# Windowed attention and a gated MLP on one core: when w_out's rows are requested, and the order of units 4 to 7 on TensorE

## The chip, the cores and the metric

The kernel runs on one core of a Trainium2 chip. The metric is device time in microseconds of one execution; lower is better. A core has five engines that run side by side, each through its own list of instructions in order: TensorE (PE in the profile; PEld is its weight load), VectorE (DVE), ScalarE (ACT), GpSimd (POOL) and SyncE (SP). They wait for one another through semaphores. DMA transfers are requested by an engine's list and carried out by 16 DMA engines that all queues share. SyncE's requests go through the profile's queue q1, GpSimd's through q0. Matmuls read SBUF and write PSUM, which has eight banks of 128 x 512 float32; VectorE and ScalarE bring results back to SBUF.

## The reference, cut to what matters

```python
# q, k, v: 4 batches x 8 heads x 768 positions x 64, float32
scores = q @ k.T / 8                       # per head
keep = (key < 4) | ((0 <= row - key) & (row - key < 128))   # 4 sinks, a window of 128
a = softmax(where(keep, scores, -1e9))
x = (a @ v), heads side by side            # 3072 tokens x 512
h = x @ w_in                               # 512 x 2048
g = h * sigmoid(beta * h)                  # beta per column
out = g @ w_out                            # 2048 x 512, float32
```

Only blocks on the band of 128 and the sinks' columns of the score matrix have to be computed.

## The kernel before, in words

**Tiles and units.** The 3072 tokens are cut into 8 tiles of 384, two per batch. The attention of a tile is done in four *units*, each one pair of heads: unit n belongs to tile n // 4. Odd tiles are the second half of a batch; their units also attend to the four sinks, for which `k_sink` and `v_sink` are kept apart. A unit needs q and k of its rows (`load_qk`, two transfers of 192 KB), cast to bf16 (`cast`), transposed on TensorE (`transpose_in`, or `transpose_first` for units 0 to 3) and copied back as `qkT`; then scores, one or two exponentials on ScalarE, a mask on VectorE (L733, L771), the product with v (`attend`, L789 and L800), division by the row sums (`normalise`, L809 and L811), and a transpose into `xT` (`transpose_out`). Units 8 and up have their results transposed by DMA, units 12 and up their inputs too (`land_qk`, `turn`).

**The MLP.** For each tile, 16 hidden blocks of 128 columns (`hidden`, L844: four matmuls of 384 columns each), a tanh on ScalarE (L852) and a product on VectorE (`gate`, L865) give g; then 3 x 16 products with w_out (`project`, L879) make the tile's 384 output rows: for each of three row groups t, sixteen blocks m are summed in one bank. The three groups use the banks acc0 and acc1 in turn. Hidden blocks need w_in, which comes in four quarters of four blocks (`load_w_in`), and products need w_out, which comes in eight transfers of two blocks (`load_w_out`). Both are cast from float32 to bf16 on the way, which is why GpSimd requests them. All of it is loaded once, during tiles 0 and 1.

**What sets the order.** The program is recorded as nodes with costs by `op`, each for one engine, and `Prog.order` plans them: for every engine it takes, of the nodes whose inputs are ready, the one that can start first, in five rounds between which the landings of DMA transfers are worked out anew (`landings`) from sizes, rates, weights and the numbers in `QUEUE`, `TAIL` and `late`. The plan only fixes the order on each engine; on the chip semaphores decide the time. Where the planner sees TensorE idle ahead of the first products, it puts in *fillers*, matmuls of ones into a bank that is free (L871). An argument `after` of a node makes it wait for the writers of the tiles named: `load_w_out(0, 2, [("w_in", 0, 12)])` waits until the last quarter of w_in has landed. `seq` keeps the loads on one queue in program order.

**The part in question** is tile 0's MLP and tile 1's attention, 17 to 50 us. SyncE requests q and k of units 4 to 7 and the float32 v of tile 1 (`load_v32`) when w_in's second quarter has landed. GpSimd casts them, casts v (`cast_v`), and between these requests w_out; it also requests the sinks' keys (`load_sink_keys`, two transfers of 8 KB into `k_rows`), which TensorE transposes (L632) into `k_sink`. Units 8 to 11 are loaded by SyncE into the stage buffers of units 0 to 3, each after one of w_out's transfers: unit n after the transfer that brings block 2n - 12. `Q_COPY` says which engine copies the transposed q of units 0 to 3 out of PSUM.

Of the kernel before, what the change touches and what calls it, by code (L numbers as in the profile page):

```python
# [9 lines left out]
B, H, S, D = 4, 8, 768, 64  # L10
NSINK, WINDOW = 4, 128
DM, DF, NOUT = 512, 2048, 512
# [6 lines left out]
TT = 384  # L19
NT = NTOK // TT  # L20
NU = 4 * NT
NM = DF // 128
# [23 lines left out]
NEG = -1.0e6  # L46
PE_MASK = 4

Q_COPY = ("act", "act", "dve", "dve")

# [319 lines left out]
def bass_streamingllm_window__then__act_swish_beta_kernel(  # L370
# [29 lines left out]
    xT = sb("xT", (128, 4, NTOK), BF16)  # L400
# [6 lines left out]
    ident = sb("ident", (128, 128), BF16)  # L407
# [6 lines left out]
    v_stage = sb("v_stage", (128, 3, H, D), F32)  # L414
# [5 lines left out]
    k_rows = sb("k_rows", (NPAIR, NSINK, 2, D), BF16)  # L420
# [19 lines left out]
    def pe(n):  # L440
        return {"busy": 2.5 + n / 2.4, "lag": 260.0}
# [7 lines left out]
    def transfer(size, rate, busy=470.0, weight=1.0):  # L449
        return {"busy": busy, "lag": size / rate, "weight": weight}  # L450
# [69 lines left out]
    def place(n):  # L520

        return n // 8, n % 4, n // 4 % 2, n % 4
# [7 lines left out]
    def load_qk(n, x, after=(), queue="sp"):  # L530
        _, _, half, pb = place(n)
        name = "qk"[x]
        s = rows_of((q, k)[x], n, 1, half, 3)
        d = stage[name][pb][:, :, 3 * half:3 * half + 3, :].rearrange("p h c d -> p h (c d)")
        op(queue, lambda e: e.dma_start(d, s), w=[(name + "_stage", pb, half)], after=after,  # L535
           dma=f"{name}{pb}_{half}", seq="loads " + queue, **transfer(2 * TT * D * 4, 330 if n < 4 else 290, 520.0))

    def load_v32(T, x, c, after=()):

        eng = "sp"  # L540
        kb = 3 * T + c
        src = v[0, 4 * x:4 * x + 4, kb * 128:kb * 128 + 128, :].rearrange("h p d -> p h d")
        op(eng, lambda e: e.dma_start(v_stage[:, c, 4 * x:4 * x + 4, :], src), w=[("v_stage", x, c)], after=after,
           dma=f"v{x}{c}", seq="loads " + eng, **transfer(4 * 128 * D * 4, 230, 520.0))

    def cast_v(n, eng="gp", after=()):
        z, T = n % 4, n // 4
        op(eng, lambda e: e.tensor_copy(v_aug[:, z, :, 3 * T:3 * T + 3, 0:D].rearrange("p h c d -> p c h d"),
                                        v_stage[:, :, 2 * z:2 * z + 2, :]),
           r=[("v_stage", z // 2, c) for c in range(3)], after=after,  # L550
           w=[("v", z, 3 * T + c, hh) for c in range(3) for hh in range(2)],
           **({"busy": 460.0, "lag": 100.0} if eng == "gp" else dve(450.0)))
# [46 lines left out]
    def load_w_out(m, ms, after=()):  # L599
        op("gp", lambda e: e.dma_start(w_out16[:, m:m + ms, :], w_out_src[:, m:m + ms, :]), after=after,  # L600
           w=[("w_out", mm) for mm in range(m, m + ms)],
           dma=f"wo{m}", **transfer(ms * 128 * NOUT * 4, 416, 740.0, 3.0))

    def load_sink_keys(after=()):
        for hh in range(2):
            src = k[:, :, 0:NSINK, :].rearrange("b (g h) s d -> h (b g) s d", h=2)[hh]
            op("gp", lambda e, hh=hh, src=src: e.dma_start(k_rows[:, :, hh, :], src),
               w=[("k_rows", hh)], after=after, dma=f"sk{hh}", busy=650.0, lag=300.0, weight=0.4)
# [18 lines left out]
    def sink_keys():  # L627

        bank16 = tr_ps[:, :].bitcast(BF16)
        with P.together("pe"):  # L630
            for s in range(NSINK):
                op("pe", lambda e, s=s: nc.tensor.transpose(  # L632
                    bank16[:, s * NPAIR:(s + 1) * NPAIR],
                    k_rows[:, s, :, :].rearrange("n h d -> n (h d)"), ident[0:NPAIR, 0:NPAIR]),
                   r=[("k_rows", 0), ("k_rows", 1), "ident"], w=["tr"], **pe(60))
        src = bank16[:, 0:NSINK * NPAIR].rearrange("x (s n) -> x n s", s=NSINK)
        for hh in range(2):
            rows = slice(64 * hh, 64 * hh + 64)
# [238 lines left out]
    def project(T, t, m, bank, name, eng="act", cols=slice(0, NOUT), queue="sp"):  # L877
# [25 lines left out]
       w=["beta_stage"], dma="beta", busy=500.0, lag=100.0)  # L903
# [6 lines left out]
    for c in range(3):  # L910
        load_v32(0, 1, c)
    op("act", lambda e: e.activation(scratch[:, :], ones32[:, 0:1], AF.Exp, bias=0.0, scale=1.0),
       r=["ones32"], w=["scratch"], busy=1500.0)
# [24 lines left out]
    cast(3)  # L938
    load_w_in(4, 4, [("k16", 0)])
    cast_v(2)  # L940
    cast_v(3)
    load_w_in(8, 4, [("v", 3, 0, 0)])
    load_w_in(12, 4, [("v", 3, 0, 0)])
    for n in range(4):
        if n < 2:
            transpose_first(n + 2)
        if n < 3:
            first_scores(n + 1)
        if n == 2:
            for y in range(4, 8):  # L950
                for x in range(2):
                    load_qk(y, x, [("w_in", 0, 4)])
                if y % 2 == 1:
                    for c in range(3):
                        load_v32(1, y // 6, c)
            masks(0, range(6), [("v", 3, 0, 0)])
            load_sink_keys([("v", 3, 0, 0)])
            load_w_out(0, 2, [("w_in", 0, 12)])
        bank = (acc[1], "acc1") if n < 3 else (h_ps[:, 0, :], "h0")
        attend(n, *bank)  # L960
        normalise(n, *bank)
# [19 lines left out]
    for s in range(-2, S_END + NM):  # L981
        i = block_of(s) if 0 <= s < S_END else None
        if i is not None:
            hidden(i, 3 if i < 2 else 0)
        if i == 2:
            P.fillers.append((filler(0), [ones_made], P.nodes[-2]))
        later = []
        for n, step in AGENDA.get(s, ()):
            if step == "in" and n < XBAR:
                transpose_in(n, eng="act" if n in (5, 7) else "dve")  # L990
            if step == "b" and n // 4 != 2:
                scores_at_once(n, 0 if n < 8 else 2)
# [12 lines left out]
        if s in casts:  # L1005
            cast(casts[s])
        if s == 3:
            for n in range(4, 8):
                cast_v(n, "gp")
        if s == 0:  # L1010
            for m in range(2, 8, 2):
                load_w_out(m, 2, [("k_stage", 1, 1)])
        if s == 2:
            for m in range(8, NM, 2):
                load_w_out(m, 2, [("k_stage", 1, 1)])
            for n in range(8, 12):
# [73 lines left out]
```

## Time and profile before

| | us |
|---|---|
| median of 3 runs | 229.56 |
| the three runs | 228.48, 229.56, 229.59 |
| the profiled execution | 228.67 |
| its span, first to last instruction | 226.7 |
| TensorE busy in the span | 215.9 |

The granted TensorE clock of the span reads 1.00. The profile gives the span alone; the profiled execution's own time is some 2 us longer, which lies around the span. In a timeline a row is a run of like instructions on one engine: start, length, engine, line, what it writes and reads, and in brackets how long the engine had been idle and what ended that. The line of GpSimd's or SyncE's request tells when a transfer was asked for, not when it landed; the time to landing is given apart. Transfers that matter here, requested and landed: w_in at 8.90, 11.68, 13.74, 14.47, landed 6.3, 6.2, 7.0 and 9.4 us later; unit 4's q at 17.85 (6.2) and k at 18.26 (6.5); the sinks' keys at 16.65 and 17.16 (7.6 and 7.3).

### The profile page before, as it was taken

What the parts mean: (1) busy time and instruction counts of PE and PEld (TensorE: products, weight loads), DVE (VectorE), ACT (ScalarE), POOL (GpSimd) and SP (SyncE); (2) the same over time, 40 slices, a digit from 0 to 9 for tenths busy, and PEclk for the clock granted to TensorE, in tenths of its full rate; (3) what the DMA queues carried; (4) which work ended last, traced back from release to release, by engine and by line L of the source; (5) the groups of instructions that cost most, each with busy time, mean ns of one, the idle gap of its engine ahead of it and who ended that gap; (6) DMA issues with size and microseconds to landing.
All of it is one profiled execution on the core that took longest, in us unless ns stands there. A gap on an engine that the chain in (4) does not pass through costs nothing.

```text
span 226.7 us, 4386 instructions
## 1 busy us (share of the span) xinstructions
PE 215.9 (95%) x1716; PEld 121.4 (54%) x1743; DVE 132.4 (58%) x261; ACT 140.4 (62%) x204; POOL 125.1 (55%) x193
## 2 busy tenths in 40 slices
PE   7899948999999999999999999999999999999995
PEld 4466625464555555555555555455555555555454
DVE  4776735558996566777766655555566563443200
ACT  3678855527776768666767676666656765555310
POOL 6681793589997697998979497877300000000000
DMA  5999999999999998999999999999901102110122
GB/s 158 262 196 200 263 247 201 239 261 158 107 117 112 166 118 116 124 130 146 172 115 154 102 138 137 123 155 136 141 20 58 53 21 64 46 49 0 61 78 93
DMA packets 98388, 29.68 MB, mean 131 GB/s; under 512 B 84912, under 2 KB 95424, under 8 KB 98368
## 3 DMA queue, kind: packets, MB, share of 16 engines
q0 software_dynamic: 55888, 10.52, 61.0%
q1 hardware_dynamic: 42304, 18.75, 37.2%
q8 instruction: 13, 0.21, 0.4%
q10 hardware_dynamic: 176, 0.14, 0.2%
q14 instruction: 7, 0.06, 0.1%
HBM read 27.32 MB, written 6.29 MB: 148 GB/s over the span
## 4 chain that ended last, share of the span: by engine, by line
PE 78%; DMA 13%; POOL 3%; SPq 2%; issue 2%; ACT 0%; ACTq 0%; POOLq 0%
PE hs_ps L844 33%; PE acc L879 32%; DMA w_out<-in_moe_w_out_dram 6%; PE hs_ps L800 4%; PE hs_ps L753 4%; DMA q_stage<-in_q_dram 3%; DMA w_in<-in_moe_w_in_dram 3%; SPq L535 2%; DMA k_stage<-in_k_dram 2%; POOL w_out L600 2%; PE hs_ps L879 2%; PE hs_ps L789 1%; PE hs_ps L719 1%; POOL qk L649 1%; PE hs_ps L742 1%
## 5 line engine op out<-in xcount | busy, mean ns | idle before, releaser
L852 ACT ACTIVATE th<-hs_ps,beta_half 128x384 f32<-128x384 f32 x120 | 68.7, 581 | 50.8 <-PE hs_ps L844 49.5
L879 PE MATMUL acc<-w_out,g 128*128 128x512 bf16 x341 | 93.1, 380 | 4.9 <-DMA w_out<-in_moe_w_out_dram 3.2
L844 PE MATMUL hs_ps<-xT,w_in 128*128 128x384 bf16 x480 | 94.4, 326 | 0.4 <-DVE g L865 0.2
L865 DVE SCALAR_TENSOR_TENSOR g<-th,hs_ps 128x384 bf16<-128x384 f32 x120 | 65.2, 551 | 35.6 <-ACT th L852 33.8
L844 PEld LDWEIGHTS hs_ps<-xT,w_in 128*128 128x128 bf16 x480 | 45.4, 98 | 35.8 <-DVE g L865 1.2
L879 PEld LDWEIGHTS acc<-w_out,g 128*128 128x128 bf16 x368 | 33.4, 98 | 34.9 <-DMA w_out<-in_moe_w_out_dram 4.4
L765 ACT ACTIVATE E<-hs_ps 128x1920 bf16<-128x1920 f32 (+1 forms) x24 | 39.9, 1661 | 4.8 <-PE hs_ps L753 4.6
L569 POOL DMA_DIRECT2D land<-in_q_dram x40 | 30.5, 766 | 15.2 <-DVE rden L809 15.2
L771 DVE TENSOR_TENSOR E<-E,mask 128x1536 bf16<-128x1536 bf16 x24 | 23.2, 967 | 26.3 <-ACT E L765 26.3
L569 POOL DMA_DIRECT2D land<-in_k_dram x40 | 30.5, 765 | 0.0
L578 POOL DMA_DIRECT2D v_aug<-in_v_dram x40 | 30.5, 764 | 0.0
L887 ACT ACTIVATE out_sb<-acc 128x512 f32<-128x512 f32 x23 | 13.6, 595 | 13.2 <-PE acc L879 13.1
L800 PE MATMUL hs_ps<-v_aug,E 128*128 128x65 bf16 x348 | 17.4, 193 | 0.1
L800 PEld LDWEIGHTS hs_ps<-v_aug,E 128*128 128x128 bf16 x348 | 15.7, 97 | 2.9 <-issue 1.6
L811 DVE TENSOR_TENSOR o_norm<-hs_ps,rden 128x384 bf16<-128x384 f32 x29 | 16.1, 557 | 1.1
L726 ACT ACTIVATE E<-hs_ps 128x768 bf16<-128x768 f32 x16 | 12.5, 807 | 2.4 <-PE hs_ps L719 2.4
L753 PE MATMUL hs_ps<-qkT 64*128 64x128 bf16 (+2 forms) x176 | 12.1, 253 | 0.0
L789 PE MATMUL hs_ps<-v_sink,E 128*128 128x130 bf16 x48 | 9.3, 219 | 0.0
L753 PEld LDWEIGHTS hs_ps<-qkT 64*128 64x128 bf16 x176 | 6.0, 94 | 5.8 <-issue 5.1
L809 DVE RECIPROCAL rden<-hs_ps 128x6 f32<-128x6 f32 x29 | 5.6, 192 | 4.7 <-PE hs_ps L800 4.7
L649 POOL CAST qk<-k_stage 128x384 bf16<-128x384 f32 x12 | 6.2, 515 | 3.0 <-DMA k_stage<-in_k_dram 2.9
L649 POOL CAST qk<-q_stage 128x384 bf16<-128x384 f32 x8 | 4.1, 517 | 6.4 <-DMA q_stage<-in_q_dram 6.4
(67 smaller groups left out, 135.5 us busy)
## 6 DMA issues: line engine op xcount, KB each, us to landing
out_dram<-out_sb SPq DMA_DIRECT2D x23, 256.0 KB, 2.6
q_stage<-in_q_dram SPq DMA_DIRECT2D x12, 192.0 KB, 5.8
k_stage<-in_k_dram SPq DMA_DIRECT2D x12, 192.0 KB, 6.0
w_in<-in_moe_w_in_dram POOLq DMA_DIRECT2D x4, 512.0 KB, 6.6
w_out<-in_moe_w_out_dram POOLq DMA_DIRECT2D x8, 256.0 KB, 9.7
land<-in_q_dram POOLq DMA_DIRECT2D x40, 48.0 KB, 3.4
land<-in_k_dram POOLq DMA_DIRECT2D x40, 48.0 KB, 3.8
v_aug<-in_v_dram POOLq DMA_DIRECT2D x40, 48.0 KB, 3.3
```

The source lines that it names most:

```text
L569: op("gp", lambda e, d=d, s=s: e.dma_start(d, s), w=[("land", pb, half, x, hh)], after=after, dma=f"l{pb}{half}{x}{hh}", **transfer(TT * D ...
L578: op("gp", lambda e, d=d, s=s: e.dma_start(d, s), w=[("v", pb, 3 * half + c, hh) for c in range(3)], after=after, dma=f"lv{pb}{half}{hh}", ...
L753: op("pe", lambda e, at=at, w=w, kb=kb, qb=qb, nq=nq, hh=hh, rows=rows, bank=bank: e.matmul(hs_ps[:, of + 2 * hh + bank, at:at + w], keys_ ...
L765: op("act", lambda e: e.activation(dst, src, AF.Exp, bias=0.0, scale=SCALE), x=list(names), w=[("E", z, 0), ("E", z, 1)], **act(1920 if ha ...
L771: op("dve", lambda e: e.tensor_tensor(E[z][:, :, 0:768], E[z][:, :, 0:768], m.unsqueeze(1).to_broadcast([128, 2, 768]), ALU.mult), r=[("E" ...
L800: last=(x == len(kbs) - 1): e.matmul(av_ps[:, at + hh * D1:at + hh * D1 + D1], E[z][:, hh, col:col + 128], v_aug[:, pb, hh, kb, 0:D1], sta ...
L811: op("dve", lambda e: e.tensor_tensor(o_norm[o][:, :, :, :].rearrange("p m h d -> p (m h) d"), src[:, :, 0:D], rden[z][:, :].unsqueeze(2). ...
L844: op("pe", lambda e: e.matmul(bank, w_in16[:, c, m * 128:(m + 1) * 128], xT[:, c, T * TT:(T + 1) * TT], start=(c == 0), stop=(c == 3)), r= ...
L852: op("act", lambda e: e.activation(th[i % 3][:, :], bank, AF.Tanh, bias=0.0, scale=beta_half[:, m:m + 1]), x=[name], r=["beta"], w=[("th", ...
L865: op("dve", lambda e: e.scalar_tensor_tensor(g[T % 2][:, m, :], th[i % 3][:, :], 1.0, bank, ALU.add, ALU.mult), r=[("th", i % 3)], x=[name ...
L879: op("pe", lambda e: e.matmul(bank[:, 0:width], g[T % 2][:, m, t * 128:(t + 1) * 128], w_out16[:, m, cols], start=(m == 0), stop=(m == NM ...
L887: op("act", lambda e: e.activation(out_sb[z][:, 0:width], bank[:, 0:width], AF.Copy, bias=0.0, scale=0.5), x=[name], w=[("out_sb", z)], ** ...
```

## The change

1. `Q_COPY`: the q of units 2 and 3 is copied by ScalarE instead of VectorE.
2. w_out's first two blocks are requested when w_in's second quarter has landed, not its last.
3. w_out's other blocks: 2 to 7 are recorded with the casts of unit 7 and may go once k of unit 6 (blocks 2 to 5) or k of unit 7 (6 and 7) has landed; 8 to 15 once the last v of tile 1 has landed. Before, all of them could go once k of unit 5 had landed.
4. The sinks' keys are requested between casts of v, ahead of w_in's last two quarters, and their transposes wait for `xT` of unit 3.
5. The loads of units 4 to 7 keep their order (written out), and those of v wait for w_in's second quarter by name. The loads of units 8 to 11 are recorded two blocks later (s == 4 instead of 2) with the same `after`.
6. The planner's numbers for these transfers change: rates, weights, and a delay of 3300 for the q of unit 4. They act through the order alone.

The order that comes out differs on every engine. On TensorE the transposes of `k_rows` go before hidden block 3, unit 4's q transposes after block 11 and its k after block 13; no filler stands after the hidden layer; 4 products with w_out precede unit 6's transposes, and 24 (instead of 48) precede the first hidden matmul of tile 1. The transposes of unit 8, which preceded it, follow it. On GpSimd: request of blocks 0 and 1, casts of units 4 and 5, casts of v, casts of unit 6, request of blocks 2 and 3, casts of unit 7, requests of 4 to 7, casts of v, requests of 8 to 15.

```diff
-Q_COPY = ("act", "act", "dve", "dve")
+Q_COPY = ("act", "act", "act", "act")
...
            dma=f"{name}{pb}_{half}", seq="loads " + queue,
-           **transfer(2 * TT * D * 4, 330 if n < 4 else 290, 520.0))
+           late=3300.0 if (n, x) == (4, 0) else 0.0,
+           **transfer(2 * TT * D * 4, 290 if n > 3 else 180 if n == 1 else 330, 520.0, 5.0 if 4 <= n < 8 else 1.0))
...
-           dma=f"v{x}{c}", seq="loads " + eng, **transfer(4 * 128 * D * 4, 230, 520.0))
+           dma=f"v{x}{c}", seq="loads " + eng, **transfer(4 * 128 * D * 4, 230, 520.0, 0.55))
...
-           dma=f"wo{m}", **transfer(ms * 128 * NOUT * 4, 416, 740.0, 3.0))
+           dma=f"wo{m}", **transfer(ms * 128 * NOUT * 4, 350, 740.0, 3.0))
...
                    k_rows[:, s, :, :].rearrange("n h d -> n (h d)"), ident[0:NPAIR, 0:NPAIR]),
-                   r=[("k_rows", 0), ("k_rows", 1), "ident"], w=["tr"], **pe(60))
+                   r=[("k_rows", 0), ("k_rows", 1), "ident"], w=["tr"], after=[("xT", 0, 3)], **pe(60))
...
     cast_v(2)
+    load_sink_keys([("k16", 0)])
     cast_v(3)
...
         if n == 2:
-            for y in range(4, 8):
-                for x in range(2):
-                    load_qk(y, x, [("w_in", 0, 4)])
-                if y % 2 == 1:
-                    for c in range(3):
-                        load_v32(1, y // 6, c)
+            load_qk(4, 0, [("w_in", 0, 4)])
...
+            load_v32(1, 1, 2, [("w_in", 0, 4)])
             masks(0, range(6), [("v", 3, 0, 0)])
-            load_sink_keys([("v", 3, 0, 0)])
-            load_w_out(0, 2, [("w_in", 0, 12)])
+            load_w_out(0, 2, [("w_in", 0, 4)])
...
+        if s == 2:
+            load_w_out(2, 2, [("k_stage", 2, 1)])
+            load_w_out(4, 2, [("k_stage", 2, 1)])
+            load_w_out(6, 2, [("k_stage", 3, 1)])
         if s == 3:
             for n in range(4, 8):
                 cast_v(n, "gp")
-        if s == 0:
-            for m in range(2, 8, 2):
-                load_w_out(m, 2, [("k_stage", 1, 1)])
-        if s == 2:
-            for m in range(8, NM, 2):
-                load_w_out(m, 2, [("k_stage", 1, 1)])
+            load_w_out(8, 2, [("v_stage", 1, 2)])
+            load_w_out(10, 2, [("v_stage", 1, 2)])
+            load_w_out(12, 2, [("v_stage", 1, 2)])
+            load_w_out(14, 2, [("v_stage", 1, 2)])
+        if s == 4:
             for n in range(8, 12):
                 for x in range(2):
                     load_qk(n, x, [("w_out", 2 * n - 12)])
```

More of the change, by code (lines that the diff above doesn't have):

```diff
@@ L535, in load_qk @@
         op(queue, lambda e: e.dma_start(d, s), w=[(name + "_stage", pb, half)], after=after,
-           dma=f"{name}{pb}_{half}", seq="loads " + queue, **transfer(2 * TT * D * 4, 330 if n < 4 else 290, 520.0))
+           dma=f"{name}{pb}_{half}", seq="loads " + queue, late=3300.0 if (n, x) == (4, 0) else 0.0,
+           **transfer(2 * TT * D * 4, 290 if n > 3 else 180 if n == 1 else 330, 520.0, 5.0 if 4 <= n < 8 else 1.0))
     def load_v32(T, x, c, after=()):
@@ L949, in bass_streamingllm_window__then__act_swish_beta_kernel @@
         if n == 2:
-            for y in range(4, 8):
-                for x in range(2):
-                    load_qk(y, x, [("w_in", 0, 4)])
-                if y % 2 == 1:
-                    for c in range(3):
-                        load_v32(1, y // 6, c)
+            load_qk(4, 0, [("w_in", 0, 4)])
+            load_qk(4, 1, [("w_in", 0, 4)])
+            load_qk(5, 0, [("w_in", 0, 4)])
+            load_qk(5, 1, [("w_in", 0, 4)])
+            load_v32(1, 0, 0, [("w_in", 0, 4)])
+            load_v32(1, 0, 1, [("w_in", 0, 4)])
+            load_v32(1, 0, 2, [("w_in", 0, 4)])
+            load_qk(6, 0, [("w_in", 0, 4)])
+            load_qk(6, 1, [("w_in", 0, 4)])
+            load_qk(7, 0, [("w_in", 0, 4)])
+            load_qk(7, 1, [("w_in", 0, 4)])
+            load_v32(1, 1, 0, [("w_in", 0, 4)])
+            load_v32(1, 1, 1, [("w_in", 0, 4)])
+            load_v32(1, 1, 2, [("w_in", 0, 4)])
             masks(0, range(6), [("v", 3, 0, 0)])
-            load_sink_keys([("v", 3, 0, 0)])
-            load_w_out(0, 2, [("w_in", 0, 12)])
+            load_w_out(0, 2, [("w_in", 0, 4)])
         bank = (acc[1], "acc1") if n < 3 else (h_ps[:, 0, :], "h0")
```

## The prediction

> **What bounds the kernel now.** I read the page first: the share of each engine and the slices, to see where TensorE has holes.
>
> ```profile
> span 226.7 us, 4386 instructions
> PE 215.9 (95%) x1716; PEld 121.4 (54%) x1743; DVE 132.4 (58%) x261; ACT 140.4 (62%) x204; POOL 125.1 (55%) x193
> PE   7899948999999999999999999999999999999995
> DMA  5999999999999998999999999999901102110122
> ```
>
> TensorE is the bound. Its only holes after the start are in slices 5 to 8 (28 to 50 us), where the DMA engines are full. A table by stretches prices them:
>
> ```profile
> 17.25:28.40 11.15, 11.15 (x79) 6.68 (x77) 8.11 (x16) 9.65 (x20) 4.73 (x9) 1.00 1.18 233
> 28.40:50.49 22.09, 18.20 (x185) 10.29 (x187) 10.90 (x20) 10.25 (x10) 14.04 (x22) 1.00 1.28 239
> 50.49:75.00 24.51, 24.04 (x214) 13.26 (x214) 19.71 (x40) 18.25 (x28) 21.48 (x31) 1.00 1.50 130
> ```
>
> The columns are stretch, length, then busy time of PE, PEld, DVE, ACT, POOL. From the end of tile 0's hidden layer (28.40) to the first hidden matmul of tile 1 (50.49) TensorE idles 22.09 - 18.20 = 3.89 us, and some 0.4 us of its busy time are fillers: at most 4.3 us can be won. After 50.49 it hardly idles. The waits of TensorE between 15 and 55 us and its timeline name the cause:
>
> ```profile
> PE acc L879 <- DMA w_out<-in_moe_w_out_dram: 3.2, 3, 1.5
> PE hs_ps L662 <- POOL qk L649: 0.5, 1, 0.5
> ```
> ```profile
> 28.35 0.54 PE L871 MATMUL acc<-ones 128*128 128x384 bf16 x3
> 30.38 0.38 PE L879 MATMUL acc<-w_out,g 128*128 128x512 bf16 x1 [1.49 <-DMA w_out<-in_moe_w_out_dram]
> ...
> 33.80 1.04 PE L879 MATMUL acc<-w_out,g 128*128 128x512 bf16 x4 [1.40 <-DMA w_out<-in_moe_w_out_dram]
> ```
>
> The first rows of w_out are late because GpSimd asks for them behind a cast that waits for q of unit 4 (timeline of POOL):
>
> ```profile
> 24.09 0.51 POOL L649 CAST qk<-q_stage 128x384 bf16<-128x384 f32 x1 [6.42 <-DMA q_stage<-in_q_dram]
> 24.54 0.73 POOL L600 DMA_DIRECT2D w_out<-in_moe_w_out_dram  x1
> 25.27 0.52 POOL L649 CAST qk<-k_stage 128x384 bf16<-128x384 f32 x1
> ```
>
> That request landed 5.6 us later, at 30.1. The remaining seven, asked for between 26.6 and 31.3, landed one after another from 33.8 to 44.3 and slowed the loads beside them. The DMA view of 32 to 36 us shows how the queues share:
>
> ```profile
> q0 software_dynamic: 641, 0.62, 91.1%
> q1 hardware_dynamic: 642, 0.16, 30.1%
> ```
>
> Packet for packet: q1's small packets of v wait behind q0's large ones. The last v of unit 7, asked for at 27.5, took 11.3 us.
>
> **The change, part by part.** Let wo0 be w_out's blocks 0 and 1, wo2 the next two, and so on.
>
> *wo0.* Its request moves from 24.54 to 17.84 (landing of w_in's second quarter), behind w_in's last two quarters on q0. It then shares the engines with the loads of unit 4. From 27 to 29 us both queues ran: q0 moved 0.20 MB, q1 0.22 MB; from 24 to 26 q1 alone moved 0.57 MB. So wo0's 256 KB take some 2.6 us, and cost q1 2.6 x (0.285 - 0.11) = 0.45 MB, or 1.6 us. q4 landed at 24.0 and k4 at 24.8; they get 0 to 1.6 us later. I take q4 24.7 (only its first part is shared) and k4 26.4 (all of it). Units 6 and 7 gain that back, since wo0 no longer sits among them: k6 landed at 30.3 and k7 at 31.5; I keep 30.5 and 31.8. The v of unit 7 no longer shares: k7 plus three loads of about 0.5, 33.2 instead of 38.8.
>
> *k_rows.* Two requests of 0.51 move ahead of w_in's last quarters, which are asked for 1.0 later (13.7 to 14.7) and wait in the queue anyway until 17.8. The two small loads took 0.4 and 0.25 behind w_in (24.25, 24.50), so w_in lands up to 0.6 later, 21.3 and 24.5; blocks 8 and 12 of the hidden layer need it at 22.7 and 25.3. The transposes of k_rows move ahead of block 3 (19.2); their data is there by 18.5. Cost 0; without that cover TensorE would wait.
>
> *The q copies of units 2 and 3* go from VectorE (0.5 each) to ScalarE (0.48), which idles 1.30 and 0.59 us just there before the exponentials; VectorE loses about 1 us of work. Between +0.5 (were they on the chain of exponentials) and -0.3: taken 0. The few fillers added in the head lie in waits for the exponentials: 0.
>
> *TensorE's order.* Before the first hidden matmul of tile 1 the new order has 24 of tile 0's 48 products instead of all 48, and unit 8's transposes behind it. Moved work is not lost: 24 x 0.216 + 0.33 = 5.5 us. So that matmul must start before 50.49 - 5.5 = 44.98 for a gain. I walk there with rows of before: hidden block 0.65, three transposes 0.17, scores 0.70, attention products 0.55, exponential (L765) 1.77, mask 0.96, copy 0.80 on ACT and 0.95 on DVE, reciprocal and normalisation 0.75, cast 0.45 and weight request 0.74 on POOL, and about 0.1 from engine to engine.
>
> Block 11 ends at 25.3, q4's cast too; k4's at 27.0 costs 0.25; the hidden layer ends at 28.5. Two products, unit 5's transposes, unit 4's scores, two products: 30.4. GpSimd now casts v (third landing 29.3) before q6 and k6, which are ready at 30.8 and 31.25: unit 6's transposes end at 31.5. Unit 5's scores use the banks of unit 4's exponential, 30.2 to 31.95: 32.05 to 32.75. Unit 4's mask ends at 32.95, its attention 33.6; unit 7's transposes wait for a DVE copy: 34.3; unit 6's scores for unit 5's exponential: 35.4; unit 5's attention ends at 36.25. wo2 follows k6's cast at 31.25. The 5.6 us of wo0 held 2.6 us of shared transfer, alone about 1.3: 4.3 us, so wo2 lands near 35.7, no wait. Four products, unit 7's scores (behind unit 6's exponential) end at 38.1, one product, attention of unit 6 at 38.9, eight products and a transpose 40.8, attention of unit 7 41.6, seven products and a transpose 43.4. That is 1.6 us of gain; 3.2 us of waits are left, now for exponentials and masks rather than weights.
>
> The Trainium skill's page "DMA: Bandwidth & Descriptors" (section "Anatomy of one DMA — SWDGE (gpsimd) path") gives 2.0 us plus bytes over 436 GB/s, which for 256 KB is an estimate of 2.6 us instead of my 4.3. The shortest row here, 5.6 us under sharing, is far above it; by the page every weight would come 1.7 us earlier and the next loss would vanish, a sum of -1.6.
>
> *Units 8 to 11.* Their loads on SP hang on the landings of wo4, wo6, wo8 and wo10; q8 was asked for at 35.42, as wo4 landed. wo4 now stands behind q7's and k7's casts, lands at 37.4, and k8, landed 43.7 before, comes at 45.2 to 45.7 and is cast by 45.8 to 46.3. TensorE, ahead of its old schedule, wants it at 45.7. Loss 0.1 to 0.65, taken 0.3. TensorE wants the later units about 2 us apart, and they land 1 us apart, as before.
>
> The sum is 1.6 - 0.3 = 1.3 us gained. The profiled execution took 228.67 us, so 227.4 by it. The median is 229.56 and the runs lie at 228.5 or 229.6; from the middle of profile and median, 229.1, I forecast 227.8.
>
> **Rivals.**
> 1. *No change to speak of.* wo0 holds q4 and k4 by the full 1.6 us and more, unit 4 and all behind it slide by 0.8, and k8 costs 0.65: gain about 0.2 to 0.5, 228.7. For it: no packet of q1 moved from 18 to 21 us though q4 was asked for at 17.85, so q0 can shut q1 out. Against: from 27 on they share evenly.
> 2. *Better.* wo0 costs unit 4 nothing, units 6 and 7 land a microsecond sooner without w_out beside them, k8 is in time: gain 2.6, 226.5. The turnaround through ScalarE (0.70 of scores, then 1.77, four times) stays, which speaks against more.
> 3. *Slower: w_out behind casts.* wo2 to wo14 now stand in GpSimd's queue behind q6 to k7 and v. If a request takes 6.2 us (the w_in rows) to 7.1 (wo2's own row) to land instead of 4.3, wo2 lands at 37.5 to 38.4, TensorE waits 1.2 to 2.1 at the products, and k8 comes 2 to 3 us later, another 1.2: 0.8 to 1.7 above the old time, 230.0 to 230.8. It decides from about 5.3 us on. Against it: those rows were taken with the queue full.
> 4. *It does nothing*, because exponentials and not weights set units 4 to 7: 229.1.
>
> **How the numbers follow.** Forecast 0.40, rivals 1 to 4: 0.26, 0.13, 0.17, 0.04. About 0.5% (1.1 us) is what a measurement of this kernel can tell from no change. The forecast lies beyond that by little, so a quarter of its chance counts as the same: faster 0.30 + 0.13 + 0.03 of rival 1 = 0.46; same 0.10 + 0.22 + 0.04 = 0.36; slower 0.17 and rounding, 0.18. The range reaches from a little past rival 2 to rival 3: 225.9 to 230.5. The forecast alone would be 227.0 to 228.6.
>
> **What would show it.** Right: wo0's wait at the first product gone and no filler behind the hidden layer; tile 1's first hidden matmul near 43.4 with half of tile 0's products behind it; between 30 and 42 us TensorE's holes ended by ACT and DVE, none by w_out. Wrong: a hole of over 0.5 us at unit 4's transposes inside the hidden layer (rival 1); products of w_out waiting near 36 us, or unit 8's transposes waiting for casts of GpSimd by more than 1 us (rival 3).

## The result and the profile after

The changed kernel took 231.51 us (median of 17 runs) and the kernel before 229.54 (17 runs beside them). The ratio is 1.0071, 95% interval 1.0047 to 1.0095: slower by 1.6 us, where 227.8, a gain, was forecast. This ratio and all others here leave out the slow runs, those over 1.5% above the fastest of their kernel (2 of the changed kernel's 17), so it is a little below that of the two medians. The profiled execution took 230.56 us, 228.8 of it the span; before it was 228.67 and 226.7.

The page after: span, busy time, and the slices of TensorE and of the DMA engines.

```profile
span 228.8 us, 4396 instructions
PE 217.9 (95%) x1721; PEld 121.4 (53%) x1749; DVE 131.6 (58%) x259; ACT 141.4 (62%) x206; POOL 125.9 (55%) x193
PE   7899979889998999999999999999999999999995
DMA  5999989999999999999999989999921112110122
```

The hole that was in slices 5 to 7 before (9, 4, 8) is nearly filled (9, 7, 9); new small ones stand in slices 8, 9 and 13. The same stretches as before, with the same columns, and one stretch more:

```profile
28.40:50.49 22.09, 19.19 (x192) 10.45 (x192) 13.62 (x26) 12.24 (x13) 19.43 (x30) 1.00 1.10 203
50.49:75.00 24.51, 22.96 (x204) 12.56 (x207) 18.64 (x38) 17.08 (x26) 21.73 (x30) 1.00 1.80 158
75.00:100.00 25.00, 24.24 (x206) 13.87 (x209) 16.42 (x31) 18.07 (x26) 21.59 (x30) 1.00 1.43 132
```

The last of these stretches in the kernel before:

```profile
75.00:100.00 25.00, 24.68 (x207) 14.33 (x210) 16.64 (x33) 18.29 (x25) 22.26 (x30) 1.00 1.24 124
```

From 28.40 to 50.49 TensorE is busy 0.99 us longer than before (19.19 against 18.20): that is the gain that the change was about. From 50.49 to 75 it does 1.08 less (22.96 against 24.04), and from 75 to 100 another 0.44 less (24.68 before). The gain is real, and about three times as much is lost afterwards, as the table below adds up. The first rows of TensorE's waits after 50 us name where:

```profile
PE hs_ps L845 <- DMA xT<-o_norm: 1.5, 2, 1.1
PE acc L880 <- issue: 0.3, 2, 0.2
```

Before, that list held nothing but waits of 0.2 us and less:

```profile
PE acc L879 <- issue: 1.0, 6, 0.2
PE hs_ps L844 <- DVE g L865: 0.2, 1, 0.2
```

`xT` is the hidden layer's input, and L845 the hidden layer's matmul. The timeline of TensorE at the start of tile 1, of tile 2 and of tile 3:

```profile
43.86 1.46 PE L845 MATMUL hs_ps<-xT,w_in 128*128 128x384 bf16 x8
45.16 0.33 PE L663 MATMUL hs_ps<-ident,qk 128*128 128x128 bf16 x3
46.06 1.04 PE L880 MATMUL acc<-w_out,g 128*128 128x512 bf16 x4 [0.57 <-DMA w_out<-in_moe_w_out_dram]
...
48.09 0.39 PE L880 MATMUL acc<-w_out,g 128*128 128x512 bf16 x1 [0.17 <-DMA w_out<-in_moe_w_out_dram]
...
70.68 0.65 PE L845 MATMUL hs_ps<-xT,w_in 128*128 128x384 bf16 x3
72.39 0.99 PE L845 MATMUL hs_ps<-xT,w_in 128*128 128x384 bf16 x5 [1.06 <-DMA xT<-o_norm]
...
94.76 0.34 PE L845 MATMUL hs_ps<-xT,w_in 128*128 128x384 bf16 x1 [0.44 <-DMA xT<-o_norm]
```

Tile 1 starts at 43.86 (50.49 before) with 24 products behind it instead of 48. Then it meets w_out's blocks 12 and 14, which landed at 46.02 and 48.04 (42.25 and 44.26 before). Tile 2 starts at 70.68 (74.64 before) with 60 products behind it instead of 80, and stops after three of the four matmuls of its first block: the fourth chunk of `xT` is unit 11's result. The chain of releases that leads to this wait runs through SyncE:

```profile
65.47 0.12 DVE rden L810
65.58 0.16 SPq L821
...
65.91 1.21 SPq L585
67.12 0.04 issue
67.16 5.19 DMA xT<-o_norm
72.35 0.05 issue
72.39 0.99 PE hs_ps L845 x5
```

Unit 11's result is ready at 66.17, waits a microsecond on SyncE behind the transposing DMA of unit 14's inputs (L585), and its own transposing DMA takes 5.19 us to land. Before, tile 2 began with eight matmuls in a row:

```profile
74.64 1.53 PE L844 MATMUL hs_ps<-xT,w_in 128*128 128x384 bf16 x8
```

The result landed at 75.13; the third of these matmuls started at 74.96, so that TensorE came to the fourth, which needs the result, at 75.12, and started it at 75.18. So there was no slack even before. Now the result lands 2.8 us sooner (72.35), but TensorE comes to it 4.0 us sooner (71.17).

To add this up I take for every hidden block the time at which it starts, less the length of all of TensorE's matmuls ahead of it but the fillers, at their usual lengths (0.1625 us a hidden matmul, 0.2162 a product, and so on, from rows of before). What is left is idle time, fillers counted in, and its difference to before tells where time is lost, however the work is ordered. After minus before:

| stretch, by hidden blocks | idle time, after minus before |
|---|---|
| up to 16, tile 1's first | -1.11 |
| 16 to 19: w_out's blocks 12 and 14 | +0.91 |
| 19 to 32: small waits in tile 1 | +0.57 |
| 32 to 33: unit 11's result | +1.17 |
| 48 to 49: unit 15's result | +0.62 |
| all | +2.16 |

The spans differ by 2.1.

### The profile page after: what moved, and what is told of

The parts are those of the page before. It is cut to its first block, busy times and chain, and to the rows that moved or that the text cites. A ratio compares the mean times of both kernels' runs of the same rounds, so it can differ in the third digit from the quotient of the medians.

```text
span 228.8 us, 4396 instructions
## 1 busy us (share of the span) xinstructions
PE 217.9 (95%) x1721; PEld 121.4 (53%) x1749; DVE 131.6 (58%) x259; ACT 141.4 (62%) x206; POOL 125.9 (55%) x193
## 4 chain that ended last, share of the span: by engine, by line
PE 68%; DMA 15%; SPq 6%; DVE 4%; POOL 3%; issue 2%; ACT 1%; ACTq 0%
PE acc L880 29%; PE hs_ps L845 28%; DMA xT<-o_norm 4%; DMA w_out<-in_moe_w_out_dram 4%; DMA k_stage<-in_k_dram 4%; SPq L535 3%; PE hs_ps L754 3%; PE hs_ps L801 3%; DMA w_in<-in_moe_w_in_dram 3%; SPq L544 2%; POOL w_out L601 2%; PE hs_ps L880 2%; DVE g L866 1%; POOL qk L650 1%; PE hs_ps L790 1%
## 5 line engine op out<-in xcount | busy, mean ns | idle before, releaser
L853 ACT ACTIVATE th<-hs_ps,beta_half 128x384 f32<-128x384 f32 x120 | 69.5, 582 | 63.7 <-PE hs_ps L845 62.8
L845 PE MATMUL hs_ps<-xT,w_in 128*128 128x384 bf16 x480 | 96.2, 326 | 2.1 <-DMA xT<-o_norm 1.5
L845 PEld LDWEIGHTS hs_ps<-xT,w_in 128*128 128x128 bf16 x480 | 45.7, 98 | 40.5 <-DMA xT<-o_norm 2.3
L650 POOL CAST qk<-q_stage 128x384 bf16<-128x384 f32 x8 | 4.7, 588 | 6.7 <-DMA q_stage<-in_q_dram 6.7
```

The costliest lines, as they stand in the source:

```text
L845: op("pe", lambda e: e.matmul(bank, w_in16[:, c, m * 128:(m + 1) * 128], xT[:, c, T * TT:(T + 1) * TT], start=(c == 0), stop=(c == 3)), r= ...
L853: op("act", lambda e: e.activation(th[i % 3][:, :], bank, AF.Tanh, bias=0.0, scale=beta_half[:, m:m + 1]), x=[name], r=["beta"], w=[("th", ...
```

## The experiments

Three theories. **A, reserve**: products with w_out are work that TensorE can do at any time; the change spends 20 of them less ahead of tiles 2 and 3 (60 instead of 80, 91 instead of 111), so TensorE gets there before the units' results. **R, requests**: w_out's late requests cost the time by themselves. **B, units**: the units 8 to 11 are late whatever the order. All times are to be read as ratios to the kernel before, run on the same chip beside each.

**1. The reserve restored (e1).** The only edit is edges in the plan between nodes of TensorE, which set an order and no wait on the chip. GpSimd's list, w_out's requests with it, comes out the same; the orders of VectorE, ScalarE and SyncE follow TensorE's in part. `products_of` holds the nodes of `project` in the order in which they are recorded, `blocks_of` those of `hidden`.

```diff
+    products_of, blocks_of = [], {}
...
+    blocks_of[32].preds[products_of[79].id] = products_of[79]
+    blocks_of[33].preds[products_of[79].id] = products_of[79]
+    blocks_of[48].preds[products_of[110].id] = products_of[110]
+    blocks_of[49].preds[products_of[110].id] = products_of[110]
```

> The changed kernel, with only TensorE's order altered: 80 products of w_out (it has 60) ahead of hidden blocks 32 and 33, the first of tile 2, and 111 (it has 91) ahead of blocks 48 and 49, the first of tile 3, the counts of the kernel before. Theory A (reserve): the two waits for a transposed result of the attention, 1.4 us at 71.0 and 0.6 us at 94.0, come because TensorE gets to those blocks with 20 products fewer behind it, 20 x 0.216 = 4.3 us sooner, than the units' chain was timed for. With the counts restored both waits vanish, the span falls by 1.5 to 2.0 us, and the time by the same: about 229.7, equal to the kernel before. Theory B (units): the units 8 to 11 themselves end later (their last v lands at 54.8), and the order only moves the wait: the products are delayed by the same amount elsewhere, and the time stays within 0.5 of the changed kernel's 231.5.

Measured: ratio 1.0004 (0.997 to 1.0038), where the changed kernel had 1.0071. The waits of TensorE from 70 us on, of this kernel:

```profile
PE acc L882 <- issue: 0.6, 4, 0.2
PE hs_ps L845 <- DVE g L867: 0.2, 1, 0.2
```

Both waits for results are gone. Theory A's number came out.

**2. The reserve taken from the kernel before (e9).** The counter-test: GpSimd's list as before, w_out's requests with it, and only edges added; 60 products ahead of tile 2 and 91 ahead of tile 3.

```diff
+    for b, k in {16: 48, 32: 60, 33: 60, 48: 91, 49: 91}.items():
+        for x in products_of[:k]:
+            blocks_of[b].preds[x.id] = x
+    for b, k in {32: 60, 33: 60, 48: 91}.items():
+        for x in products_of[k:k + 48]:
+            x.preds[blocks_of[b].id] = blocks_of[b]
```

> The kernel before, w_out's requests and all untouched, with only TensorE's order altered: 60 products instead of 80 ahead of blocks 32 and 33, and 91 instead of 111 ahead of 48, the counts of the changed kernel (48 ahead of tile 1 stay). In the kernel before, unit 11's transposed result landed at 75.13 and TensorE came to block 33 at 75.35; with 20 products fewer ahead it comes some 4 us sooner. Theory A (reserve): it now waits for that result, 1 to 4 us, and again up to 0.6 for unit 15's, and the time rises to 1.005 to 1.018 of the kernel before. Theory R (the requests alone cost the time): no change, within 0.3%.

Measured: ratio 1.0173 (1.0117 to 1.0229). The first rows of TensorE's waits after 50 us of this kernel:

```profile
PE hs_ps L844 <- DMA xT<-o_norm: 1.8, 2, 1.0
PE hs_ps L719 <- DVE qkT L669: 0.4, 1, 0.4
PE hs_ps L789 <- DVE E L771: 0.3, 1, 0.3
```

The order alone, without any change to w_out's requests, makes the kernel slower than the change did (six runs), and with the same wait. By the same reckoning as in the table above, the ledger from here on, it loses 1.6 us at block 33 (1.2 of it the wait for unit 11's result), 1.0 at block 49 and 1.8 between blocks 16 and 31, where only 12 products are left among the units' steps (32 before). So the reserve also covers small waits inside tile 1. Theory R's "no change" is out; that the late requests cost nothing is not thereby shown.

**3. Unit 11's result without the DMA (g1).** One result is transposed by TensorE; the order is otherwise kept but for one product (59 and 90 ahead of tiles 2 and 3).

```diff
-        if n >= XBAR_OUT:
+        if n >= XBAR_OUT and n != 11:
...
-            if step == "out" and n < XBAR_OUT:
+            if step == "out" and (n < XBAR_OUT or n == 11):
```

> The changed kernel with one step done otherwise: unit 11's result is transposed by TensorE (three transposes of 0.06 us and a copy of 0.28 on VectorE) and not by SyncE's transposing DMA, which took 5.19 us from request to landing. TensorE's counts stay: 24, 59 and 90 products ahead of tiles 1, 2 and 3. Theory A (the little reserve shows the DMA's latency): the wait of 1.1 to 1.4 us at block 33 goes without any reserve added, that of 0.6 at tile 3 stays, the transposes cost 0.2: ratio 1.002 to 1.005. Theory B (the unit's arithmetic itself is late): a wait for VectorE or TensorE of the same size stands there instead, ratio 1.006 or more.

Measured: ratio 0.9993 (0.9961 to 1.0026). No wait for `xT` is left in the list of this kernel, at tile 3 neither, and three transposes stand between products ahead of tile 2:

```profile
70.17 0.81 PE L880 MATMUL acc<-w_out,g 128*128 128x512 bf16 x3
70.82 0.33 PE L829 MATMUL hs_ps<-ident,o_norm 128*128 128x128 bf16 x3
71.20 0.81 PE L880 MATMUL acc<-w_out,g 128*128 128x512 bf16 x3
```

In this trace tile 1 began 2.1 us later than in the trace after (45.93), so a wait could be missing for that reason alone. It is not so: unit 11's result was ready at 67.92, and with the 6.2 us that it took from there to its landing in the trace after, it would have come at 74.1 by this estimate, while TensorE was there at 72.88. The unit's arithmetic is in time, then; theory B falls, and the DMA's latency is the cause that the missing reserve lays bare. I expected 1.002 to 1.005, with tile 3's wait left; that went too, though unit 15 still goes through the DMA, which took 4.08 us here instead of 5.05, while TensorE came 0.5 us later. SyncE's list is one transposing DMA shorter; that this is the reason is not shown.

**4. SyncE's queue (e4).** The transposing DMA of unit 11's result (`out_of`, the nodes of `transpose_out`) goes ahead of that of unit 14's inputs (`turn_of`, those of `turn`).

```diff
+    turn_of[14].preds[out_of[11].id] = out_of[11]
```

> The changed kernel, with SyncE's transposing DMA of unit 11's result ahead of that of unit 14's q and k, behind which it waited 1.0 us (66.17 ready, 67.16 issued). TensorE's order follows: 56 products instead of 60 ahead of block 32. Theory A: the result lands by up to 1.0 us sooner, TensorE comes 4 products = 0.9 us sooner too, so the wait of 1.4 us at block 33 stays within 0.5 of that and the time at 231.0 to 231.7. Theory C (the order of SyncE's queue is the cause): the wait falls to 0.4 and the time to 230.5.

Measured: ratio 1.0038 (1.0007 to 1.0069). In its trace the wait at tile 2 is down from 1.17 to 0.43 and that at tile 3 is gone. It lies between what the two theories expected, and its interval overlaps that of the changed kernel. Unit 11's result is requested 0.03 us after it is ready, where it had waited 0.99, so the place in SyncE's queue has a part. But the DMA also took 4.01 us instead of 5.19, and TensorE came 1.4 us sooner after the result was ready than in the trace after; how much of the change is the queue's, this run doesn't settle.

**5. Half the reserve (g2).** As the first, with 70 products ahead of blocks 32 and 33 and 101 ahead of 48 and 49, and at most 24 ahead of block 17.

> The changed kernel with half of the reserve restored: 70 products ahead of blocks 32 and 33 and 101 ahead of 48, 2.2 us each. The waits it has to cover were 1.1 to 1.4 and 0.6 us in the changed kernel's trace. Theory A: both go, ratio 0.999 to 1.002, the same as with the whole reserve (1.0004). If the reserve works in another way than by covering these two waits, the ratio lies half-way, 1.003 to 1.005.

Measured: ratio 1.001 (0.9974 to 1.0046), and no wait for `xT` in the trace: unit 11's result landed at 72.19, and TensorE came to it at 75.08. Half is enough.

**6. w_out's late rows (e2, e3).** The first product with block 12 goes behind hidden block 19, the first with block 14 behind block 21; once with the changed kernel's counts, once with the reserve.

```diff
+    products_of[24].preds[blocks_of[19].id] = blocks_of[19]
+    products_of[28].preds[blocks_of[21].id] = blocks_of[21]
```

> The changed kernel, with only two products moved in TensorE's order: the first product with w_out's block 12 behind hidden block 19, the first with block 14 behind block 21 of tile 1. Those rows land at 46.0 and 48.0 and TensorE waits 0.57 and 0.17 us and some more for them. Theory A: these waits vanish, 0.7 to 0.9 us, but TensorE then reaches tile 2's first block still earlier with respect to unit 11's result, so the wait there grows by what was won: time 231.5, unchanged within 0.4. Theory B (w_out's late rows are the loss themselves): the time falls by 0.7 to 0.9, to 230.7.

> Both edits at once: 80 and 111 products ahead of tiles 2 and 3, and the products with blocks 12 and 14 behind blocks 19 and 21. Theory A (reserve, and late rows): neither wait is left, the idle time of the changed kernel falls by 2.1 to 2.7 us, and the gain of 1.1 us at the first block of tile 1 reaches the end: 228.5 to 229.3, 0.3 to 1.0 below the kernel before. Theory B (something later binds, the units' chain or the last tile): 229.7 or more.

Measured: 1.0064 (1.0027 to 1.0101) without the reserve, 0.9961 (0.9925 to 0.9996) with it. Without it, the waits after 50 us begin with this row, 1.9 us in one wait where the changed kernel had 1.5 in two:

```profile
PE hs_ps L845 <- DMA xT<-o_norm: 1.9, 1, 1.9
```

The time is unchanged, as theory A said, and the waits at w_out's rows are gone. That what was won there is waited for at tile 2, this trace does not show: TensorE came to the place at 71.28 (71.17 in the trace after), and the wait is longer because unit 11's DMA took 6.26 us instead of 5.19. With the reserve the time fell below that of the kernel before, by 0.4%; whether it is a gain, the set under 8 has to say.

**7. The requests (e5, e6, e7, e10, e11, e12).** First, w_out's first rows alone, in the kernel before:

```diff
-            load_w_out(0, 2, [("w_in", 0, 12)])
+            load_w_out(0, 2, [("w_in", 0, 4)])
```

> The kernel before with one edit: w_out's blocks 0 and 1 are asked for at w_in's second landing, as in the change, and nothing else. TensorE keeps its reserve of 48, 80 and 111 products ahead of tiles 1, 2 and 3. The wait of 1.49 us for these rows at 30.4 should vanish. Theory A: the wait is won only as far as the next rows allow (they land at 33.8, where TensorE waited 1.40 us, and it now comes 1.5 sooner): the first hidden matmul of tile 1 moves from 50.5 by 0 to 0.5, and the time by as much, 229.0 to 229.6. Theory D (this request costs the loads of units 4 to 7 their share of the queues): slower, 230 or more.

Measured: ratio 1.0003 (0.9962 to 1.0043). Waits of TensorE from 28 us on:

```profile
PE acc L879 <- DMA w_out<-in_moe_w_out_dram: 2.9, 1, 2.9
```

The two waits of 1.5 and 1.4 became one of 2.9 for the next rows: nothing won, as expected. Second, the changed kernel with w_out's requests where they had been (the lines of the diff that move `load_w_out` undone); the plan then puts 46, 77 and 111 products ahead of tiles 1 to 3.

> The changed kernel with w_out's requests back where the kernel before had them (blocks 0 and 1 behind w_in's last landing, the others behind casts of units 4 to 6); the planner's figures stay as changed, and TensorE's order has 46 products ahead of tile 1. If the requests are what costs time (rows 12 and 14 landing at 46.0 and 48.0 instead of 42.3 and 44.3, v of units 8 to 10 3 us later), the time comes back to 229.5 or below. If the order by the planner's new figures costs it, it stays at 231 or above.

Measured: ratio 0.996 (0.9931 to 0.999). The loss goes, but the reserve has come back with the requests, so this does not tell A from R. Third, the other half: requests as changed, and 48, 80 and 111 products.

> The changed kernel with the three counts of the kernel before: 48, 80 and 111 products ahead of tiles 1, 2 and 3, with w_out's requests as changed. Theory A (reserve): the waits for unit 11's and unit 15's results vanish; but TensorE must now take the products of blocks 12 and 14 before tile 1, and their rows land at 46.0 and 48.0, so it cannot start tile 1 before 48.0 plus what is left, about 50 to 51: 229.3 to 230.5, below the changed kernel. If it stays at 231.5, the order has nothing to do with it.

Measured: ratio 1.0077 (1.0036 to 1.0117); theory A's 229.3 to 230.5 was wrong. TensorE has to take blocks 12 and 14 before tile 1 here, waits 1.27 us for w_out at 45.55 and 1.22 for unit 8's cast at 47.16, and is then slowed by the clock (below); tile 1 starts at 57.77. So the late rows do cost time where the order needs them early. Fourth to sixth: the old requests with 24 products ahead of tile 1, then 60 and 91 (e10) or 80 and 111 (e11), and e11 with the first rows early (e12), by the same loops as under 2, which also hold 30, 36 and 40 products ahead of blocks 20, 24 and 28.

> The changed kernel with w_out's requests where the kernel before had them, and TensorE's counts held at those of the changed kernel: 24, 60 and 91 products ahead of tiles 1, 2 and 3. Beside the same requests with 46, 77 and 111 products (ratio 0.996). Theory A (reserve): the wait for unit 11's result is there, 1 to 2 us, and the ratio is 1.002 to 1.008. Theory R (the requests): no such wait, ratio 0.996 as before or below.

> The same requests as in the kernel before, with 24, 80 and 111 products ahead of tiles 1, 2 and 3: tile 1 early, the reserve kept ahead of tiles 2 and 3. Theory A: both waits gone, w_out's last rows land at 42 to 44, before they are wanted, and the gain at tile 1 stays: ratio 0.990 to 0.996, the best of all. Theory B (the units' chain ends later however the products are ordered): no better than 0.996.

> As the last, with w_out's blocks 0 and 1 asked for at w_in's second landing too. If the first rows' wait of 1.49 us at 30.4 is worth something once tile 1 starts early, the ratio falls by another 0.002 to 0.005, to 0.987 to 0.993; if the next rows' landing at 33.8 takes its place, as it did with only that request moved, it is that of the last, within 0.002.

Measured: 1.0047 (1.0 to 1.0094) and 1.0044 (1.0006 to 1.0083); for e12 no ratio, as its runs lie from 229.4 to 237.0. The medians of all runs of e10 and e11, 233.3 and 231.9 beside 230.1 before, lie further up than the ratios say, because in most of these runs the clock fell (below). Expected was that the reserve tells e10 from e11, and it doesn't: neither shows a wait for unit 11's result. Both lose their time earlier. The waits of TensorE between 28 and 75 us in e10:

```profile
PE hs_ps L801 <- POOL v_aug L549: 2.0, 1, 2.0
PE hs_ps L829 <- DVE o_norm L812: 1.8, 2, 0.9
PE acc L882 <- DMA w_out<-in_moe_w_out_dram: 1.7, 2, 1.2
```

With the old requests unit 7's v lands late (its cast could start only at 43.31), and the 24 products that would have stood in those gaps were held back by my edges. Tile 1 starts at 48.6 and 48.5 in these two, where the changed requests let it start at 43.86; whether another order could start it early with the old requests was not tried.

**8. What of the gain can be had (f1 to f4).** All have 80 and 111 products ahead of tiles 2 and 3. f1 holds tile 1's products to w_out's landings (at most 20 ahead of block 17, 24 ahead of 19, 28 ahead of 20, 31 ahead of 22); f2 is f1 with this line; f3 is this line with at most 24 products ahead of block 17; f4 is f1 with the edge of e4.

```diff
-                    load_qk(n, x, [("w_out", 2 * n - 12)])
+                    load_qk(n, x, [("w_out", 2 * n - 12 + 2 * (n >= 9))])
```

> The changed kernel with 80 and 111 products ahead of tiles 2 and 3, and with TensorE's products at tile 1 held to w_out's landings: 20 ahead of block 16 (blocks up to m = 9), 24 by block 19, 28 by block 20. Theory A (reserve first, then late rows): with the reserve alone the ratio was 1.0004, with rows 12 and 14 moved behind tile 1's first blocks 0.9961, and there waits of 0.6 us for rows 8 and 10 were left; without these 0.993 to 0.997. Theory B (TensorE then waits for unit 7's result instead): block 16 no earlier than 43.9, ratio 0.996 to 1.000.

> As the last, with the loads of q and k of units 9, 10 and 11 asked for one landing of w_out later each (behind rows 8, 10 and 12 instead of 6, 8 and 10). If the queue that w_out shares with them delays its last rows, those land 1 to 2 us sooner than 46.0 and 48.0; the units then end about 1 us later, which the reserve of 80 products covers. Ratio 0.001 to 0.003 below the last where the rows still cost time, 0.002 or more above it where the units' chain has no slack.

> The changed kernel with 24, 80 and 111 products ahead of tiles 1, 2 and 3 and the later loads of units 9 to 11, the products at tile 1 otherwise as the planner puts them. Against the kernel with the reserve alone (ratio 1.0004): if w_out's last rows are what was left of the loss, the waits for rows 12 and 14 go, and the ratio is 0.995 to 0.998.

> The kernel with products held to w_out's landings and the reserve kept, and SyncE's transposing DMA of unit 11's result ahead of unit 14's. With 80 products ahead of tile 2 that result lands some 4 us before it is wanted, so the order of SyncE's queue is worth nothing: the ratio of the first of this set within 0.002. If it is lower by more, the chain of units 12 to 15 or that of tile 3 still binds.

Measured: 0.9999 (0.9965 to 1.0034), 1.0012 (0.998 to 1.0043), 0.9986 (0.9951 to 1.0022), 0.999 (0.9961 to 1.0019). f1 has the ratio of its theory B, though block 16 came at 43.33, sooner than B had it. f2 gains nothing: block 12 still landed at 46.07, and TensorE waits up to 1.7 us for a cast of the units' inputs. f3's blocks 12 and 14 landed a microsecond sooner (44.93 and 46.98), but its ratio stayed above the 0.995 to 0.998 expected, though its interval reaches that far. f4 is f1's equal, as expected. Tile 1 starts at 43.1 to 44.4 in these traces, early as planned, and the time is still that of the kernel before. The ledger, relative to before, shows where it goes, one execution to a column:

| blocks | after | e1 | f1 | f3 | f4 | g1 |
|---|---|---|---|---|---|---|
| 15 to 16 | -1.03 | -0.66 | -1.02 | -1.33 | -0.77 | -0.24 |
| 16 to 20 | +0.90 | +0.25 | +0.08 | +0.19 | -0.05 | +0.59 |
| 20 to 32 | +0.58 | +1.16 | +0.96 | +0.57 | +0.94 | +0.58 |
| 32 to 36 | +1.17 | -0.08 | -0.07 | -0.07 | -0.07 | -0.07 |
| 36 to 60 | +0.61 | 0.00 | -0.03 | -0.03 | -0.03 | -0.01 |

The last two rows are the loss, and every cure takes them away whole. The first three add up to between -0.6 (f3, whose trace is the fastest of its twelve runs) and +0.9 us (g1): an early tile 1 leaves little or nothing of its gain. In blocks 20 to 32 each loses 0.6 to 1.2 us in pieces, of which the list of waits shows few over 0.3 us; what they are is left open. e3's 0.9961 has four relatives at 0.9986 to 1.0012, so I don't call any of these faster than the kernel before; nor e6, whose 0.996 no other kernel here repeats.

**9. The q copies (e8).** On VectorE again (`Q_COPY` as before).

> The changed kernel with the q copies of units 2 and 3 on VectorE again. They were costed at nothing: 231.5 within 0.4. Off by more, in either direction, would say that this part has a share in the loss or hides a gain.

Measured: ratio 1.0081 (1.0044 to 1.0119), no different from 1.0071. Costed at nothing, and worth nothing.

## Why the prediction was wrong, step by step

*wo0 and the loads of units 4 to 7: right.* q4 landed at 24.59 (forecast 24.7), k4 at 26.18 (26.4), k6 at 30.95 (30.5), k7 at 32.15 (31.8), unit 7's v at 33.66 (33.2, and 38.80 before). Rival 1, wo0 shutting out unit 4, did not happen.

*The walk to tile 1: right but for 0.5 us.* wo2 landed at 35.06 (forecast 35.7) and nothing waited for it; TensorE's holes up to 42 us end at VectorE, ScalarE and casts of GpSimd. The first hidden matmul came at 43.86 (forecast 43.4); 0.41 of the difference is a wait for block 10 at 42.82. Gain 1.11, not 1.6.

*Units 8 to 11: the wrong thing was costed.* The 0.3 was for k8, and k8, at 44.76, was sooner than the 45.2 to 45.7 forecast. What TensorE did wait for was w_out's blocks 12 and 14: I followed wo2 and left out wo10 to wo14, which share the DMA engines with the units' loads (785 packets of q0 and 789 of q1 from 44 to 48 us) and landed 5.7, 8.2 and 9.6 us after their requests. They cost 0.9. Another 0.57 went in small waits of tile 1, for which the sum had no term.

*"Moved work is not lost": the step that failed.* As a sum of work it holds. But I took 24 products moved past tile 1's start as equal to the time they take, and walked no further than unit 8. A product is also cover: 20 of them fewer ahead of tile 2 bring TensorE there 4.3 us before it would otherwise come, and the trace of before had no slack at that place (landed 75.13, wanted at 75.12). The sentence "After 50.49 it hardly idles" told of the kernel with 80 products ahead of tile 2, and I used it as if it told of the stretch. "They land 1 us apart, as before" was true of the loads and said nothing of the results. Cost 1.17 + 0.61 = 1.8 us; e1 and g1, which take away the one or the other cause, both give back the whole loss.

*Rival 3, slower, 230.0 to 230.8: its sign and not its reason.* It wanted w_out's requests to take 6.2 to 7.1 us. They took 3.6 and 3.8 for wo2 and wo4, and nothing waited for these. My 4.3 us was too much: these two took 3.50 to 3.62 us in the traces of f1 and f3. The Trainium skill's page "DMA: Bandwidth & Descriptors" (section "Anatomy of one DMA — SWDGE (gpsimd) path") gave an estimate of 2.6 us for the 256 KB that land; for the 512 KB of float32 that are read, the same fit gives an estimate of 3.2 us. The fastest of all transfers of w_out in the traces here took 3.50 us, 0.9 and 0.3 us above these two.

## What to carry to other kernels

When a bound engine has work that fits anywhere, that work is a reserve against every later latency: before letting it go for an early start, find for each later stage when the engine would arrive and when its input lands, and compare the slack with the shift. A gap in one stage of a busy engine is closed by work taken from another stage's cover, so the walk has to go on until the old and the new order have done the same work again. And a short wait of a late stage can be removed at its own cause (here one result's transposing DMA), more cheaply than by moving the whole order.

## What the runs showed of the hardware

*A lightly used TensorE pays twice.* In e11 TensorE worked 1.51 of the 3.42 us up to 47.04, and the granted clock then halved. The trace is cut below where its clock changes, and into equal stretches from there. Columns: stretch, length, busy time of PE, PEld, DVE, ACT and POOL, granted clock, DMA share, GB/s.

```profile
40.21:43.62 3.41, 1.82 (x11) 0.78 (x8) 0.96 (x1) 1.11 (x1) 0.30 (x2) 1.00 1.25 226
43.62:47.04 3.42, 1.51 (x31) 1.26 (x31) 1.73 (x5) 0.00 (x0) 1.82 (x4) 1.00 1.45 239
47.04:50.45 3.41, 2.71 (x14) 1.42 (x15) 0.49 (x2) 0.45 (x1) 3.41 (x6) 0.50 1.55 215
50.45:53.87 3.42, 3.42 (x12) 1.03 (x11) 1.97 (x3) 1.03 (x3) 3.42 (x6) 0.50 1.17 79
53.87:57.28 3.41, 3.41 (x27) 1.82 (x25) 2.51 (x5) 2.48 (x5) 3.41 (x6) 1.00 1.41 120
```

It stayed at 0.50 for 6.8 us. TensorE was busy 6.1 us of them, so it did about 3 us of work less. Full clock came back at the end of the first stretch that was busy throughout; the 0.79 of the stretch before was not enough. In the traces of e5, e6, e7, e8, e10 and e12 the clock also fell, for one or two stretches of 3.41 us, each time after one in which TensorE was busy 0.34 to 0.49 of the time, and it came back after one that was busy throughout. The least busy stretches without a fall behind them had 0.48 (e2) and 0.53 (e11, the first row), so the border lies near one half in these traces. The Trainium skill's page "TensorE: Matmul & The Clock Gate" (section "Part 1: The HAM clock gate") has the clock halve after an idle window of about 3.4 us and come back after a busy one. The length of the stretches, the halving and the return agree; but the stretch ahead of the fall need not be idle, and the longest single wait in e11 was 1.93 us.

The kernel before falls as well. Of its 150 runs beside the experiments, 74 read a granted clock of 0.997 or more over the span (229.8 us in the mean), 53 read 0.991 to 0.993, as one stretch at half clock gives (230.1), and 23 read 0.984 to 0.989, as about two give (231.2). The changed kernel reads below 0.997 in 3 of 17 runs only, so its loss is not the clock's.

*The transposing DMA's time varies.* The six that carried results and were requested between 60 and 80 us in the trace after took 3.1, 4.3, 3.9, 5.2, 3.7 and 4.0 us from request to landing; over all traces here they took 2.3 to 6.7 us. The planner counts 1.84. An order planned with that number can put TensorE at tile 2 sooner than the result is there.
